# Pacing one queue's gathers and scatters in a fused attention and expert kernel

## The chip, the cores and the metric

The kernel runs on one core of a Trainium2 chip. The metric is the device time of one execution in microseconds (us); lower is better. The engines are named as in the profile: PE (TensorE; PEld is its weight load), DVE (VectorE), ACT (ScalarE), POOL (GpSimd) and SP (SyncE, which here issues most of the transfers).

## The reference

Two blocks run one after the other. The first is attention in which a query sees only the keys of its own cluster. The second sends every token to one of eight experts. Cut to what matters:

```python
# q, k, v: (4, 8, 768, 64); centroids: (8, 16, 64)
q_assign = argmax(normalized(q) @ normalized(centroids).T)   # same for k
mask = q_assign[..., :, None] == k_assign[..., None, :]
scores = where(mask, q @ k.T / sqrt(D), -1e9)
x = softmax(scores) @ v                                # -> (3072, 512)
logits = normalized(x) @ normalized(expert_emb).T / tau  # 8 experts
e = argmax(logits)
gate = softmax(logits)[e]
out = gate * (relu(x @ w1[e]) @ w2[e])                 # w1 512x1024, w2 1024x512
```

## The kernel before, in words

**Attention.** The loop runs over 16 pairs of heads (4 batches b times 4 pairs nb) and, within each, six iterations `it`. An iteration handles two units, each a block of keys against 384 queries of both heads. It makes the scores of the two units ahead (L571, into PSUM tiles `s_ps`), takes their exponentials on ACT (L582, into one of six tiles `prob`), and multiplies the exponentials of its own two units with the values (L593). DVE adds the exponentials up (L612), POOL spreads inverse sums (L664). Finished rows go to a DRAM tensor `x_rows` in transfers that SP issues (L703).

**Early experts.** Tokens of the first batches are known before attention ends. The kernel forms four "early" items E0[0] to E0[3] of 128 tokens each and works them while the last routing is done. A table `early`, keyed by (b, nb, it), says in which iteration a piece of this is recorded. `fetch(E0[0])` gathers the first item with one instruction; for the other three, `early_lot(j, n, behind)` issues the next n of the four gathers of item j. Each gather (L1144, an indirect DMA on POOL) brings 128 pieces of 512 bytes, 64 KB, into an `xin` tile. If `behind` is given, POOL first copies one element of it, so that the gathers are held until that tile has been written. After attention, `hidden(item, (half,))` multiplies with w1 (L1386, tile `h_ps`) and evicts half of `hT` on ACT (L1393); `result` multiplies with w2 (L1426) and ACT scales by the gate into `y` (L1437), which POOL scatters to the output (L1155). `turn_x` transposes a gathered item on DVE (L1262). `fetch_gate` gathers the gates of the early items.

**Routing of the rest.** Beside the early items the last batch is routed: `choose` picks experts, `pb.ranks` (from L873), `pb.dest`, `pb.hot_blocks` and their successors place the tokens. POOL's L1024 is one step of it, read by PE in L1040.

**Later items.** `later` holds sixteen items, numbered 0 to `LAST` = 15: "block" items of 128 tokens and "sized" ones, called wide here, of 160 to 272 tokens of one expert each. The wide item of number i = 12 has six 32-token pieces, that of i = 14 has five; i = 13 and i = 15 are blocks. For a wide item, `sized_hidden` makes eight tiles of hidden features (L1293), evicted by ACT into `hTs` (L1300); `sized_result` makes the output columns (L1331), which DVE transposes into `ys` (L1340) and scales (L1355). `sends` gives the scatters of `ys`, one per piece, 64 KB each (L1155). A list `queue` holds due gathers and scatters of all items. `pump(n, behind)` issues the next n behind a one-element copy on POOL (`pace`, L1683); `share(i, left, behind)` calls it with an n that spreads what is due over the slots that are left.

**The conditional region.** Within block i = 13, between the two halves of its `result`, `overflow` records a branch (L1732) on a value that is loaded on each engine. Its body handles tokens that fit in no item. With these inputs the body is skipped.

**Order.** The order on every engine is the order in which the program records instructions; nothing is reordered by a scheduler. Each engine works its own list in order and waits on semaphores of the others. [...]

Of the kernel before, what the change touches and what calls it, by code (L numbers as in the profile page):

```python
# [9 lines left out]
F32 = mybir.dt.float32  # L10
# [29 lines left out]
def kernel(  # L40
# [12 lines left out]
    nc = tc.nc  # L53
# [4 lines left out]
    F = moe_w1.shape[2]  # L58
    N = B * S
    NJ = S // P  # L60
    NHP = H // 2
# [85 lines left out]
    smp = ctx.enter_context(tc.tile_pool(name="smp", bufs=2))  # L147
# [7 lines left out]
    at = ctx.enter_context(ExitStack())  # L155
# [387 lines left out]
    un = [dict() for _ in units]  # L543
# [597 lines left out]
    mo = {}  # L1141
# [35 lines left out]
    def expert_of(it):  # L1177
        table = {"early": e_early, "sized": e_sized, "block": e_block, "whole": e_block}[it.kind]
        return nc.values_load(
            table[0:1, it.j : it.j + 1], engines=(EngineType.SP,), min_val=0, max_val=E - 1  # L1180
        )

    def weights1(it, parts=1):
        it.e = expert_of(it)
        for i in range(parts):
            load_part(w1s[it.slot], moe_w1, it.e, KD, i, parts)
# [5 lines left out]
    def load_part(w, x, e, chunks, i, parts):  # L1192
        c = slice(chunks // parts * i, chunks // parts * (i + 1))
        nc.sync.dma_start(
            out=w[:, c], in_=x[ds(e, 1)].rearrange("o (c p) f -> p (o c) f", p=P)[:, c]
        )
# [49 lines left out]
    def turn_x(it, evict=None, xT=None):  # L1246
        d = mo[it]
        if it.kind == "sized":
            n = WIDE[it.j]
            d["xT"] = szp.tile([P, KD, SQ * max(WIDE)], F32, tag="xTs", name="xTs")  # L1250
            for u in range(0, n, NQ):
                m = min(NQ, n - u)
                nc.vector.transpose(
                    d["xT"][:, :, SQ * u : SQ * u + SQ * m].rearrange(
                        "p c (w t) -> p w c t", t=SQ
                    ),
                    d["xs"][:, u : u + m].rearrange("p w (c i) -> p w c i", i=SQ),
                )
            return
        d["xT"] = mop.tile([P, DM], F32, tag="xTm", name="xTm") if xT is None else xT  # L1260
        if it.kind == "block" or it in E0[1:]:
            nc.vector.transpose(  # L1262
                d["xT"].rearrange("p (c w t) -> p w c t", c=KD, t=SQ),
                d["xin"].rearrange("p w (c i) -> p w c i", i=SQ),
            )
            return
        bk = psX.tile([P, DM], F32, tag="x_ps", name="x_ps")
        for c in range(KD):
            nc.tensor.transpose(
                bk[:, P * c : P * c + P], d["rows"][:, c].rearrange("p w i -> p (w i)"), ident  # L1270
            )
        evict(d["xT"], bk)
# [86 lines left out]
    def sends(it):  # L1359

        u0, ys = FIRST[it.j], mo.pop(it)["ys"]
        return [
            lambda u=u: scatter(
                out_pieces, flat(spidx)[:, u0 + u : u0 + u + 1], ys[:, u], NQ * N
            )
            for u in range(WIDE[it.j])
        ]

    def flat(t):
        return t.rearrange("p k w -> p (k w)")  # L1370

    def hidden(it, halves=(0, 1)):

        d = mo[it]
        for half in halves:
            if half == 0:
                d["hT"] = (
                    flat(szp.tile([P, KF, max(CAPS)], F32, tag="hTs", name="hTs", bufs=1))[:, 0:F]
                    if it.kind == "whole"
                    else mop.tile([P, F], F32, tag="hT", name="hT")  # L1380
                )
            f0 = 512 * half
            bk = psH.tile([P, 512], F32, tag="h_ps", name="h_ps")
            for m in range(0, 512, P):
                for c in range(KD):
                    nc.tensor.matmul(  # L1386
                        bk[:, m : m + P],
                        lhsT=w1s[it.slot][:, c, f0 + m : f0 + m + P],
                        rhs=d["xT"][:, P * c : P * c + P],
                        start=(c == 0),  # L1390
                        stop=(c == KD - 1),
                    )
            nc.scalar.activation(d["hT"][:, f0 : f0 + 512], bk, ACTF.Relu)  # L1393
# [21 lines left out]
    def result(it, halves=(0, 1)):  # L1415
# [44 lines left out]
        (3, 2, 3): lambda: fetch(E0[0]),  # L1460
        (3, 2, 5): lambda: order_x(E0[0]),
        (3, 3, 1): pa.spread_pieces,
        (3, 3, 2): lambda: early_lot(1, 2),
        (3, 3, 3): lambda: early_lot(1, 1),
        (3, 3, 4): lambda: early_lot(1, 1),
        (3, 3, 5): lambda: early_lot(2, 1),
    }
    early_jobs = {}

    def early_lot(j, n, behind=None):  # L1470

        if j not in early_jobs:
            early_jobs[j] = fetches(E0[j])
        if behind is not None:
            nc.gpsimd.tensor_copy(pace, behind)
        for job in early_jobs[j][0:n]:
            job()
        del early_jobs[j][0:n]
# [9 lines left out]
    E0 = items[0:KA]  # L1488
    later = items[KA:]
# [70 lines left out]
    with tc.manual_schedule(engines=by_hand):  # L1560
        begin()
        for i in range(0, len(units), 2):
            n, it = divmod(i // 2, NJ)
# [18 lines left out]
            b, nb = divmod(n, NHP)  # L1582
# [36 lines left out]
        pace = mop.tile([1, 1], F32, tag="pace", name="pace", bufs=1)  # L1619
# [2 lines left out]
        pb = Places(1, rtb)  # L1622
        gates = gate_pieces(0, B - 1)
        gates[0]()
        early_lot(2, 1)
        logits(0)
        hidden(E0[0], (0,))
        turn_x(E0[1])
# [6 lines left out]
        gates[1]()  # L1635
        gates[2]()
        hidden(E0[0], (1,))
        turn_x(E0[2])
        gates[3]()
        early_lot(3, 2, mo[E0[0]]["hT"][0:1, F - 1 : F])  # L1640
        weights1(E0[2])
        read(0, NJ, P - SQ, P)
        products(1)
        hidden(E0[1], (0,))
        logits(1)
        choose()
        early_lot(3, 2, mo[E0[1]]["hT"][0:1, 511:512])
        hidden(E0[1], (1,))
        weights1(E0[3])
        pb.ranks()  # L1650
        pb.firsts()
# [22 lines left out]
        queue = []  # L1674
# [6 lines left out]
        def pump(n, behind=None):  # L1681
            if n and queue and behind is not None:
                nc.gpsimd.tensor_copy(pace, behind)  # L1683
            queue.sort(key=lambda j: j[0])
            for due, job in queue[0:n]:
                job()
            del queue[0:n]

        def share(i, left, behind=None):

            due = len([j for j in queue if j[0] <= i])
            pump(max(-(-due // left), -(-len(queue) // (left + 3))), behind)
# [59 lines left out]
        LAST = len(later) - 1  # L1752
# [4 lines left out]
        for i, it in enumerate(later):  # L1757
            if i == LAST - 1:
                weights1(later[LAST])
                weights2(later[LAST])  # L1760
            wide = it.kind == "sized"
            if wide:
                order_w2(it)
            if i > 1 and i + 1 < len(later):
                turn_x(later[i + 1])
            made = None
            if i > 0 and later[i - 1].kind == "sized":
                made = mo[later[i - 1]]["ys"][0:1, 0, 0:1]
                queue.extend((min(i + 1, LAST - 2), f) for f in sends(later[i - 1]))
            if 0 < i < LAST - 1 and later[i + 2].kind == "sized":  # L1770
                jobs_of(later[i + 2], i)
            for k in range(i + 2, i + 4):
                if wide and block(k) and later[k] not in mo:
                    jobs_of(later[k], i)
            if wide:
                sized_hidden(it, lambda f, x: share(i, 7 - f // 2, x) if f % 2 else None)
                if i == 1:
                    turn_x(later[2])
                if i + 2 < LAST:
                    weights1(later[i + 2])  # L1780
                    weights2(later[i + 2])
                sized_result(it, lambda g, x: share(i, 3 - g, x) if g < 3 else None)
            elif i < LAST:
                share(i, 3, made)
                hidden(it, (0,))
                share(i, 2, mo[it]["hT"][0:1, 511:512])
                hidden(it, (1,))
                share(i, 1, mo[it]["hT"][0:1, F - 1 : F])
                if i == 0:
                    turn_x(later[1])  # L1790
                    pb.gates(slot_gates)
                if i + 2 < LAST:
                    weights1(later[i + 2])
                result(it, (0,))
                if i == LAST - 2:
                    overflow()
                result(it, (1,))
                if i == 0:
                    jobs_of(later[2], 1)
                    spread_gates()  # L1800
                if i + 2 < LAST:
                    weights2(later[i + 2])
            else:
                pump(len(queue))
                nc.gpsimd.drain()  # L1805
                hidden(it)
                result_last(it)
# [43 lines left out]
```

## Time and profile before

| what | us |
|---|---|
| median of three runs | 698.12 (696.0 to 698.7) |
| the profiled execution, time | 695.11 |
| the profiled execution, span | 693.0 |
| PE busy in the span | 682.6 |
| DVE busy | 382.8 |
| ACT busy | 262.2 |
| POOL busy | 275.6 |

The profile is of one execution. Its page gives busy times, the costliest groups of instructions and the chain that ended last. The trace behind it answers further questions: waits (who waited for whom, in total, how often, longest), timelines (start, duration, engine, line, operation, count, and in brackets the idle time before with what ended it), and stretches of time with the busy time of each engine, the number of its instructions, the clock granted to PE as a share of full speed (1.00 in all stretches but the last), the share of time in which the DMA engines were busy and the rate in GB/s. Line numbers are those of the kernel before. The scatter or gather instruction on POOL is 1.0 us long in the page (56 scatters at 997 ns, 56 gathers at 1013 ns); the copy of one element is 0.18 us. "POOLq" and the like is an engine's sequencer, and "remote" is a wait whose end the trace can't put down to an instruction.

Attention ends at about 325 us of the span, the early items run from there to about 392, and the block with the conditional region is worked from 640 to 660.

### The profile page before, as it was taken

How to read it: one execution, taken by the hardware profiler on the slowest of the kernel's cores; microseconds unless marked ns; L12 is line 12 of the kernel's file. 1: busy time of each engine (PE TensorE's matmuls, PEld its weight loads, DVE VectorE, ACT ScalarE, POOL GpSimd, SP SyncE). 2: the span in 40 equal slices, each digit the busy share in tenths (PEclk: the TensorE clock that was granted, in tenths of full speed). 3: DMA queues.
4: the chain of work that ended last, by engine and by line, in shares of the span. 5: the costliest groups of instructions: out<-in, count | busy, mean ns of one | idle time of the engine just before them, and what ended most of it. 6: DMA issues, size and time to landing. Idle time of an engine off the chain costs nothing. (4 is left out here: it accounts for less than half of the span.)

```text
span 693.0 us, 16339 instructions
## 1 busy us (share of the span) xinstructions
PE 682.6 (99%) x6521; PEld 460.4 (66%) x6521; DVE 382.8 (55%) x673; ACT 262.2 (38%) x444; POOL 275.6 (40%) x505
## 2 busy tenths in 40 slices
PE   8999999999999999999999999999999999999987
PEld 4544444444544444445866678888979797979785
DVE  6898998999899999997674122140301203030310
ACT  6665665576566765574242120101010101111011
POOL 2221222322131222343526343676756465647403
PEclk9999999999999999999999999999999999999999
DMA  9757755776678687689699957457787686878630
GB/s 147 121 82 116 114 100 86 153 141 106 108 131 163 139 147 142 171 209 292 175 311 388 372 189 268 147 175 279 281 282 280 202 301 231 306 249 310 242 133 33
DMA packets 244956, 135.55 MB, mean 196 GB/s; under 512 B 208640, under 2 KB 208642, under 8 KB 244876
## 3 DMA queue, kind: packets, MB, share of 16 engines
q1 hardware_dynamic: 238540, 121.29, 65.0%
q0 software_dynamic: 6160, 13.12, 5.6%
q8 instruction: 53, 0.87, 0.5%
q14 instruction: 27, 0.22, 0.1%
q10 hardware_dynamic: 176, 0.05, 0.0%
HBM read 115.93 MB, written 13.12 MB: 186 GB/s over the span
## 5 line engine op out<-in xcount | busy, mean ns | idle before, releaser
L582 ACT ACTIVATE prob<-s_ps 128x768 f32<-128x768 f32 x192 | 154.0, 814 | 104.7 <-PE s_ps L571 98.6
L571 PE MATMUL s_ps<-qT,kT 64*64 64x384 f32 x1536 | 156.9, 483 | 0.0
L593 PE MATMUL o_ps<-prob,v 64*64 64x385 f32 x1536 | 143.3, 484 | 0.6 <-issue 0.6
L612 DVE TENSOR_TENSOR acc<-acc,prob 128x768 f32<-128x768 f32 x128 | 121.5, 949 | 8.9 <-ACT prob L582 0.5
L593 PEld LDWEIGHTS o_ps<-prob,v 64*64 64x64 f32 x1536 | 58.6, 133 | 66.4 <-issue 58.1
L1340 DVE STREAM_TRANSPOSE ys<-y_ps 128x256 f32<-128x256 f32 (+4 forms) x16 | 6.1, 403 | 154.4 <-PE y_ps L1331 126.6
L1386 PEld LDWEIGHTS h_ps<-xTm,w1s 128*128 128x128 f32 x768 | 87.3, 192 | 2.0 <-issue 1.6
L1386 PE MATMUL h_ps<-xTm,w1s 128*128 128x128 f32 x768 | 88.3, 276 | 0.0
L571 PEld LDWEIGHTS s_ps<-qT,kT 64*64 64x64 f32 x1536 | 55.7, 133 | 35.9 <-issue 31.7
L1426 PE MATMUL y_ps<-w2s,hT 128*128 128x512 f32 x176 | 77.8, 594 | 0.3 <-PEq L1732 0.3
L1293 PE MATMUL h_ps<-xTs,w1s 128*128 128x272 f32 (+7 forms) x384 | 72.9, 346 | 1.8 <-ACT hTs L1300 1.8
L627 POOL COPY behind<-acc 1x1 f32<-1x1 f32 x30 | 6.7, 222 | 168.3 <-DVE acc L612 159.5
L1293 PEld LDWEIGHTS h_ps<-xTs,w1s 128*128 128x128 f32 x384 | 66.7, 190 | 8.6 <-issue 2.9
L1393 ACT ACTIVATE hT<-h_ps 128x512 f32<-128x512 f32 x24 | 14.3, 596 | 147.3 <-PE h_ps L1386 107.8
L1155 POOL DMA_INDIRECT out_dram<-ys,spidx x56 | 55.8, 997 | 33.9 <-issue 19.5
L571 PE MATMUL s_ps<-hot 64*64 64x384 bf16 x768 | 64.6, 325 | 0.1
L1144 POOL DMA_INDIRECT xs<-x_rows,gpidx x56 | 56.8, 1013 | 18.7 <-issue 18.7
L1426 PEld LDWEIGHTS y_ps<-w2s,hT 128*128 128x128 f32 x176 | 32.5, 190 | 37.4 <-issue 36.3
L571 PEld LDWEIGHTS <-hot 64*64 64x64 bf16 x768 | 24.2, 106 | 43.4 <-issue 41.5
L1331 PE MATMUL y_ps<-hTs,w2o 128*128 128x272 f32 (+7 forms) x256 | 48.0, 346 | 0.0
L1331 PE MATMUL misc<-hTs,w2o 128*128 128x272 f32 (+7 forms) x256 | 48.0, 346 | 0.0
L664 POOL COPY inv<-inv 32x12 f32<-32x12 f32 x120 | 31.5, 262 | 36.8 <-DVE inv L661 32.6
(285 smaller groups left out, 740.3 us busy)
## 6 DMA issues: line engine op xcount, KB each, us to landing
w1s<-in_moe_w_dram SPq DMA_DIRECT2D x18, 2048.0 KB
w2s<-in_moe_w_dram SPq DMA_DIRECT2D x18, 2048.0 KB
q<-in_q_dram SPq DMA_DIRECT2D x64, 96.0 KB
k<-in_k_dram SPq DMA_DIRECT2D x64, 96.0 KB
v<-in_v_dram SPq DMA_DIRECT2D x120, 48.0 KB
x_rows<-xb SPq DMA_DIRECT2D x60, 96.0 KB
xr<-x_rows SPq DMA_DIRECT2D x9, 512.0 KB
w1s<-in_moe_w_dram SPq DMA_DIRECT2D x4, 1024.0 KB
```

The lines of the kernel that those rows point to most:

```text
L571: nc.tensor.matmul(s_ps[D * half : D * half + D, h, 0:HS], lhsT=l[rows, half], rhs=r[rows], start=part == (1 if len(parts) < 2 else 0), st ...
L582: nc.scalar.activation(d["prob"][:, :, 0:HS], d["s_ps"][:, :, 0:HS], ACTF.Exp, scale=scale)
L593: nc.tensor.matmul(g["o_ps"][D * h : D * h + D, half, 0:HE], lhsT=ld[n]["v"][keys, j, h], rhs=d["prob"][keys, h, 0:HE], start=(j == 0), st ...
L612: nc.vector.tensor_tensor(g["acc"], g["acc"], d["prob"][:, :, 0:HS], ALU.add)
L664: nc.gpsimd.tensor_copy(inv2[M * to : M * to + M, :, i % 2], inv[M * i : M * i + M])
L1144: nc.gpsimd.indirect_dma_start(out=to, out_offset=None, in_=of, in_offset=bass.IndirectOffsetOnAxis(ap=at, axis=0), bounds_check=n - 1, oo ...
L1155: inst = nc.gpsimd.indirect_dma_start(out=to, out_offset=bass.IndirectOffsetOnAxis(ap=at, axis=0), in_=of, in_offset=None, bounds_check=n - 1,
L1293: nc.tensor.matmul(bk, lhsT=w1s[it.slot][:, c, P * f : P * f + P], rhs=d["xT"][:, c, 0:C], start=(c == 0), stop=(c == KD - 1),)
L1331: nc.tensor.matmul(bks[g][:, 0:C], lhsT=d["w2"][:, f, P * g : P * g + P], rhs=d["hT"][:, f, 0:C], start=(f == 0), stop=(f == KF - 1),)
L1386: nc.tensor.matmul(bk[:, m : m + P], lhsT=w1s[it.slot][:, c, f0 + m : f0 + m + P], rhs=d["xT"][:, P * c : P * c + P], start=(c == 0), stop ...
L1393: nc.scalar.activation(d["hT"][:, f0 : f0 + 512], bk, ACTF.Relu)
L1426: nc.tensor.matmul(bk, lhsT=d["hT"][:, P * c : P * c + P], rhs=w2s[it.slot][:, c], start=(c == 0), stop=(c == KF - 1),)
```

## The change

The change moves gathers and scatters on POOL to other places and puts copies ahead of some of them.

- In the last attention iterations, item 1's four gathers are recorded in iterations 2 to 5, one in each, and each behind a copy that reads the `prob` tile of the first of the iteration's own units. Before, they were recorded as 2, 1 and 1 in iterations 2, 3 and 4, without a copy.
- The first two gathers of item 2 were recorded in iteration 5 and right after attention. All four now go in two pairs, behind the first and the second half of item 0's `hT`.
- Item 3's pairs stood behind item 0's second half and item 1's first half. They now stand behind item 1's first and second half.
- The transpose of item 2 moves behind `choose` on DVE.
- Of the six scatters of the wide item i = 12, two stay in block i = 13, ahead of the region, and four fall due in the wide item i = 14, where `share` spreads them behind its `hTs` tiles. The two later `share` calls of block i = 13 go.
- The copies of `early_lot` write a small tile of a pool that exists in attention, `behind`, and no longer `pace`.

```diff
@@ -1460,11 +1460,13 @@
         (3, 2, 3): lambda: fetch(E0[0]),
         (3, 2, 5): lambda: order_x(E0[0]),
         (3, 3, 1): pa.spread_pieces,
-        (3, 3, 2): lambda: early_lot(1, 2),
-        (3, 3, 3): lambda: early_lot(1, 1),
-        (3, 3, 4): lambda: early_lot(1, 1),
-        (3, 3, 5): lambda: early_lot(2, 1),
+        **{(3, 3, it): lambda it=it: early_lot(1, 1, ahead(3, 3, it)) for it in (2, 3, 4, 5)},
     }
+
+    def ahead(b, nb, it):
+
+        return un[2 * (NJ * (NHP * b + nb) + it)]["prob"][0:1, 0, 0:1]
+
     early_jobs = {}
 
     def early_lot(j, n, behind=None):
@@ -1472,7 +1474,8 @@
         if j not in early_jobs:
             early_jobs[j] = fetches(E0[j])
         if behind is not None:
-            nc.gpsimd.tensor_copy(pace, behind)
+            at = smp.tile([1, 1], F32, tag="behind", name="behind", bufs=1)
+            nc.gpsimd.tensor_copy(at, behind)
         for job in early_jobs[j][0:n]:
             job()
         del early_jobs[j][0:n]
@@ -1622,7 +1625,6 @@
         pb = Places(1, rtb)
         gates = gate_pieces(0, B - 1)
         gates[0]()
-        early_lot(2, 1)
         logits(0)
         hidden(E0[0], (0,))
         turn_x(E0[1])
@@ -1635,17 +1637,18 @@
         gates[1]()
         gates[2]()
         hidden(E0[0], (1,))
-        turn_x(E0[2])
         gates[3]()
-        early_lot(3, 2, mo[E0[0]]["hT"][0:1, F - 1 : F])
+        early_lot(2, 2, mo[E0[0]]["hT"][0:1, F - 1 : F])
         weights1(E0[2])
         read(0, NJ, P - SQ, P)
         products(1)
         hidden(E0[1], (0,))
         logits(1)
         choose()
+        turn_x(E0[2])
         early_lot(3, 2, mo[E0[1]]["hT"][0:1, 511:512])
         hidden(E0[1], (1,))
+        early_lot(3, 2, mo[E0[1]]["hT"][0:1, F - 1 : F])
         weights1(E0[3])
         pb.ranks()
         pb.firsts()
@@ -1766,7 +1769,8 @@
             made = None
             if i > 0 and later[i - 1].kind == "sized":
                 made = mo[later[i - 1]]["ys"][0:1, 0, 0:1]
-                queue.extend((min(i + 1, LAST - 2), f) for f in sends(later[i - 1]))
+                due = LAST - 1 if i == LAST - 2 else min(i + 1, LAST - 2)
+                queue.extend((due, f) for f in sends(later[i - 1]))
             if 0 < i < LAST - 1 and later[i + 2].kind == "sized":
                 jobs_of(later[i + 2], i)
             for k in range(i + 2, i + 4):
@@ -1781,11 +1785,16 @@
                     weights2(later[i + 2])
                 sized_result(it, lambda g, x: share(i, 3 - g, x) if g < 3 else None)
             elif i < LAST:
-                share(i, 3, made)
+                if i == LAST - 2:
+                    pump(2, made)
+                else:
+                    share(i, 3, made)
                 hidden(it, (0,))
-                share(i, 2, mo[it]["hT"][0:1, 511:512])
+                if i < LAST - 2:
+                    share(i, 2, mo[it]["hT"][0:1, 511:512])
                 hidden(it, (1,))
-                share(i, 1, mo[it]["hT"][0:1, F - 1 : F])
+                if i < LAST - 2:
+                    share(i, 1, mo[it]["hT"][0:1, F - 1 : F])
                 if i == 0:
                     turn_x(later[1])
                     pb.gates(slot_gates)
```

## The prediction

> **What bounds the kernel now.** I read the page's engine totals first, then TensorE's own list of waits, then the timelines of the two places that the change touches.
>
> ```profile
> PE 682.6 (99%) x6521; PEld 460.4 (66%) x6521; DVE 382.8 (55%) x673; ACT 262.2 (38%) x444; POOL 275.6 (40%) x505
> ```
>
> TensorE (PE) is busy for 682.6 of 693.0 us. POOL issues every gather and scatter and is 40% busy. So an edit to POOL's order can only pay where PE stands still or runs below its own rate. Both touched places have such a spot. The first is the end of attention; PE's waits between 280 and 420 us are two:
>
> ```profile
> PE x_ps L1269 <- ACT prob L582: 0.9, 1, 0.9
> PE o_ps L593 <- issue: 0.6, 1, 0.6
> ```
>
> The timelines there, POOL, PE and ACT in turn:
>
> ```profile
> 316.59 1.00 POOL L1144 DMA_INDIRECT xin<-x_rows,early_i  x1 [0.30 <-issue]
> 317.89 1.00 POOL L1144 DMA_INDIRECT xin<-x_rows,early_i  x1 [0.30 <-issue]
> 319.19 1.00 POOL L1144 DMA_INDIRECT xin<-x_rows,early_i  x1 [0.30 <-issue]
> ```
> ```profile
> 317.08 1.52 PE L571 MATMUL s_ps<-qT,kT 64*64 64x384 f32 x8
> 318.10 2.31 PE L593 MATMUL o_ps<-prob,v 64*64 64x385 f32 x13
> 320.98 0.87 PE L593 MATMUL o_ps<-prob,v 64*64 64x385 f32 x3 [0.57 <-issue]
> 322.71 0.63 PE L1269 MATMUL x_ps<-ident,rows 128*128 128x128 f32 x4 [0.86 <-ACT prob L582]
> ```
> ```profile
> 321.06 1.51 ACT L582 ACTIVATE prob<-s_ps 128x768 f32<-128x768 f32 x2 [3.77 <-remote]
> ```
>
> The eight score matmuls take 1.52 us here and 0.81 or 0.82 us in every group before; the sixteen L593 matmuls take 3.75 us (318.10 to 321.85) instead of 1.46; the exponential at 321.06 starts 3.77 us after ACT fell idle, though its scores were done by 317.1. From 317.08 to the next group, at 324.72, is 7.64 us. At the pitch of the neighbours (0.65 + 1.30 + 0.56 + 1.45) it is 3.96. PE lost **3.7 us**, most of it counted as busy. POOL issues six gathers without a break just then (312.32 to 320.19), and the transfers are dense. Density alone doesn't do it, as two stretches of 4 us show (PE's matmuls are the first number in brackets; DMA share and GB/s are last):
>
> ```profile
> 304.00:308.00 4.00, 4.00 (x64) 2.02 (x60) 3.59 (x8) 2.38 (x5) 1.89 (x5) 1.00 1.03 381
> ...
> 316.00:320.00 4.00, 4.00 (x39) 1.66 (x37) 1.46 (x2) 1.29 (x3) 3.09 (x4) 1.00 1.04 374
> ```
>
> 64 matmuls against 39, at equal transfer. The gathers are what differs most visibly; the trace does not prove them the cause.
>
> The second place is the conditional region, L1732. POOL, ACT and PE:
>
> ```profile
> 650.49 0.98 POOL L1155 DMA_INDIRECT out_dram<-ys,spidx  x1 [0.57 <-issue]
> 651.77 0.97 POOL L1155 DMA_INDIRECT out_dram<-ys,spidx  x1 [0.30 <-DVE xTm L1262]
> 660.64 0.98 POOL L1155 DMA_INDIRECT out_dram<-y,sidx  x1 [7.90 <-ACT hTs L1300]
> ```
> ```profile
> 659.68 0.69 ACT L1437 ACTIVATE y<-y_ps,slot_gates 128x512 f32<-128x512 f32 x1 [10.07 <-DMA xin<-x_rows,gpidx]
> ```
> ```profile
> 654.33 3.42 PE L1293 MATMUL h_ps<-xTs,w1s 128*128 128x160 f32 x24
> 657.59 1.25 PE L1293 MATMUL x_ps<-xTs,w1s 128*128 128x160 f32 x8
> 660.61 3.53 PE L1293 MATMUL h_ps<-xTs,w1s 128*128 128x160 f32 x24 [1.77 <-ACT hTs L1300]
> ```
>
> and what POOL did in its 7.9 us, from the view of line L1732:
>
> ```profile
> L1732 POOLq EVENT_SEMAPHORE  x5: 17/42/43, 651.9 to 658.0; - x5
> ...
> L1732 POOLq INC_SWDGE_SEM  x1: 1390/1390/1390, 658.1 to 658.1; - x1
> ```
>
> The program, read from its instructions: on the path that skips the region, POOL waits until all it has sent has landed, then raises the semaphores as the skipped body would have (1.39 us, to 659.46). ACT's y waits for those semaphores and starts at 659.68. The label "xin" on its wait is an inference of the view; POOL's semaphore step is what ended just before. With y stuck, the four hTs tiles behind it on ACT stay in PSUM, and PE waits **1.77 us**.
>
> [...] the scatter at 651.77 lasts 0.97 us, and POOL is held until 658.0. [...] The trace shows up to 6.2 (651.77 to 658.0) beside weight loads, and I use 6.2. [...]
>
> **The change, part by part.** The sums are against the profiled execution: 695.11 us, 693.0 of it span. The median of the three runs, 698.12, is 3.0 above it; I carry the difference over.
>
> *Scatters.* Of six scatters of the last-but-one wide item, those at 643.36 and 644.70 stay ahead of the region; four go, with four copies of 0.18 us, behind hTs tiles 1, 3, 5, 7 of the item after it. POOL loses two pace copies ahead of the region and gains four behind it. The second scatter lands by 644.70 + 6.2 = 650.9, POOL's step ends at 652.3. ACT's y needs its matmuls, done at 650.82 + 3.67 = 654.49. So POOL is 2.2 us early, y starts at about 654.5 and hTs at 655.2, and PE's wait goes: **-1.8 us**. From there PE runs unbroken to 688, so the end moves with it. What is late next is the scores' own pace, no wait. The four scatters cost POOL 4 x (0.18 + 0.5 gap + 1.0) = 6.7 us between about 656 and 665, where it idles until 675.4. Their 262 KB are 0.7 us of DMA at the 389 GB/s of this stretch. The last weights, issued at 654.52, are needed at 679 and the DMA share is 0.06 from 670 to 680, so ten us cover this. Cost 0; without that cover, 0.7. The output buffer of the wide item behind the region is not the one that the four scatters read, so its transposes don't wait for them.
>
> *Gathers in attention.* Six in a row become four, each behind a copy that reads the score tile of its turn. POOL is inside L664 until 312.05, so the first three still go at about 312.8, 314.5 and 316.1 (0.18 copy, 0.5 gap, 1.0 each). The fourth waits for the exponential at 321.06 (or 317.9, if that is no longer held). The other two leave the stretch. I take half of the 3.7 us: **-1.8 us**, bounds -3.7 (the burst is all of it) and 0 (weights and row stores are). A loss is bounded by the cover: the gather lands at worst at 322.6 + 1.0 + 5 = 328.6; the transpose that reads it, now at 327.17, has 2.37 us of idle behind it on DVE, to 330.20. One new wait: the exponential that rewrites the first tile waits for POOL's read, done by 312.6 against 317.1. Cost 0.
>
> *Gathers of items 2 and 3.* Item 2's four go at the two existing turns, 330.77 and 336.43. Item 3's move one turn later, and its last pair goes behind the second hT half of item 1, at 342.7. That pair now issues at 343.9 and 345.2, so the four gate gathers behind it on POOL start at 346.5 instead of 343.51. ACT's y of item 0 waits for the first: 343.51 to 350.26 is 6.75 us, so 353.3. Its scatter then starts at 354.2 and POOL's L1024 at 355.5, ending 357.1. PE reads that at 359.54 (L1040): 2.4 us cover. Cost 0; each us beyond is one us.
>
> *Moved transpose.* On DVE item 2's transpose (0.71) moves behind ten small operations, to just before L873. DVE idles 4.42 us there; gathers issued by 338.8 must land by 341.5 for it. The pair issued then before had the same time. Gates come 0.2 to 0.4 us earlier. Taken as 0. SP's and PE's orders are the same in both programs. POOL gains seven copies, 1.3 us, in idle time.
>
> Sum: -1.8 - 1.8 = -3.6. Profiled 691.5; median **694.5**.
>
> **The rivals.** About 0.5%, 3.5 us, is what a measurement of this kernel can tell from no change.
> 1. *Both places pay*, with about half or more of the 3.7: 692.6 to 694.6, centre 694.5. For it: equal transfer, different matmul rate. Against: three gathers still come close together. 0.46.
> 2. *Only the region pays*; attention's end is held by the weight loads and row stores that the change leaves: 698.1 - 1.8 = 696.3, with a little from attention 695. For it: ACT was already 1.37 us late at 315.87, with two gathers issued. 0.36.
> 3. *Nothing moves*: y at 654.5 is held by another of its semaphores, or PE waits a little later: 698. Against: y starts 0.2 us after POOL's step. 0.06.
> 4. *Slower*: the delayed gate gathers reach PE. The place is L1040 at 359.54, through ACT's y and POOL's L1024. It starts to cost from a gate landing of 6.75 + 2.4 = 9.2 us. To end 3.5 us slower, with the region's gain alone, PE must stand 5.3 us, a landing of 14.5: 701.6. For it: rows are being read back there, and the 6.75 is long. Against: that reading thins out at 350. 0.12.
>
> **How the numbers follow.** Faster 0.46, same 0.36 + 0.06, slower 0.12. The forecast is rival 1's, 694.5; its own range is 692 to 695. Low end: 692.6, less 1.1 for the spread of the runs (696.0 to 698.7). High end: 698.1 for rival 3, plus 0.9. That leaves out rival 4 and some of each tail.
>
> **What would show it.** Right: no wait of PE on L1300's tiles near 659 and ACT's y at about 652 to 655; more than 39 matmuls in the 4 us from 316, and ACT's wait ahead of the last exponentials under 2 us; L1040 without a wait. Wrong: the 3.7 us at the same place with four gathers (rival 2); y still after POOL's step (3); a new PE wait between 355 and 365 (4).

## The result, and the profile after

| | median, us | runs |
|---|---|---|
| before | 698.49 | 6, 696.0 to 699.3 |
| after | 690.33 | 6, 690.0 to 692.3 |

The ratio is 0.9891, with a 95% interval of 0.9873 to 0.9910: 8.2 us faster. The forecast was 694.5, and its range ended at 691.5. The profiled execution of the changed kernel took 690.58 us with a span of 688.4; that of the kernel before took 695.11 with 693.0. So 4.6 us of the 8.2 can be looked for in the two traces. Most of the rest, 3.4 us, is that the median of the kernel before lies that far above its profiled execution. Later runs on five chips show what the number depends on: the changed kernel takes about 690 us on the two where it ran, the kernel before 695.2 to 695.8 on three and 690 on the other two.

The engine totals on the page of the changed kernel:

```profile
PE 681.5 (99%) x6521; PEld 459.7 (67%) x6521; DVE 384.0 (56%) x673; ACT 262.7 (38%) x444; POOL 277.4 (40%) x512
```

In TensorE's list of waits both waits near the end of attention and the wait on `hTs` (1.77 us before) are gone; the largest one left is 1.1 us at the start of the program.

**End of attention.** The timelines of POOL, PE and ACT of the changed kernel:

```profile
312.87 1.03 POOL L1144 DMA_INDIRECT xin<-x_rows,early_i  x1 [0.15 <-POOL behind L1478]
314.74 1.17 POOL L1144 DMA_INDIRECT xin<-x_rows,early_i  x1 [0.15 <-issue]
316.95 1.02 POOL L1144 DMA_INDIRECT xin<-x_rows,early_i  x1 [0.16 <-issue]
319.32 1.02 POOL L1144 DMA_INDIRECT xin<-x_rows,early_i  x1 [0.54 <-issue]
```
```profile
317.52 0.81 PE L571 MATMUL s_ps<-qT,kT 64*64 64x384 f32 x8
318.17 1.46 PE L593 MATMUL o_ps<-prob,v 64*64 64x385 f32 x16
319.56 0.66 PE L1269 MATMUL x_ps<-ident,rows 128*128 128x128 f32 x4
320.14 1.52 PE L593 MATMUL o_ps<-prob,v 64*64 64x385 f32 x16
321.60 0.62 PE L722 MATMUL misc<-xT,embT 128*32 128x96 f32 x20
```
```profile
317.65 1.57 ACT L582 ACTIVATE prob<-s_ps 128x768 f32<-128x768 f32 x2 [1.27 <-POOL behind L1478]
```

The eight score matmuls take 0.81 us and the sixteen L593 matmuls 1.46, as everywhere else. From the last score group to L722 it is 321.60 - 317.52 = 4.08 us; before it was 324.72 - 317.08 = 7.64. **3.56 us are gained here.** I call this the stretch below. ACT's wait fell from 3.77 to 1.27 us. The copy named as its releaser ended at 316.8, the scores that ACT takes only at 317.5, so it is the scores that it waits for. Of the four copies on POOL only the last waited for its tile (0.62 us); the second and the third lasted 0.67 and 0.87 us instead of 0.18. That is how the gathers came to start 1.9 to 2.4 us apart, where before it was 1.3 to 1.6. The window beside the one of before that the prediction shows (PE's matmuls in the first bracket, DMA share and GB/s last):

```profile
316.00:320.00 4.00, 4.00 (x48) 1.71 (x44) 3.96 (x4) 2.56 (x6) 2.67 (x4) 1.00 1.05 379
```

PE has 48 matmuls in it instead of 39, and DVE works 3.96 of 4 us instead of 1.46, at much the same 379 GB/s (374 before).

**The region.** POOL, ACT and PE, and POOL's semaphore step on the skipped path (L1732 before, now L1735):

```profile
640.85 1.03 POOL L1155 DMA_INDIRECT out_dram<-ys,spidx  x1 [0.16 <-issue]
642.18 1.00 POOL L1155 DMA_INDIRECT out_dram<-ys,spidx  x1 [0.30 <-issue]
```
```profile
652.09 0.69 ACT L1437 ACTIVATE y<-y_ps,slot_gates 128x512 f32<-128x512 f32 x1 [6.86 <-PE y_ps L1426]
```
```profile
651.84 3.42 PE L1293 MATMUL h_ps<-xTs,w1s 128*128 128x160 f32 x24
655.10 1.25 PE L1293 MATMUL x_ps<-xTs,w1s 128*128 128x160 f32 x8
656.18 3.42 PE L1293 MATMUL h_ps<-xTs,w1s 128*128 128x160 f32 x24
```
```profile
L1735 POOLq INC_SWDGE_SEM  x1: 1310/1310/1310, 644.5 to 644.5; - x1
```

POOL raises the semaphores from 644.5 to 645.8 and y now waits for nothing but its own matmuls. As the prediction reads the program, POOL's step starts when all that it has sent has landed; by that reading the second scatter (642.18) took at most 2.3 us. PE's three groups follow each other without a gap: **1.77 us gained**. The two places make 5.3 us; about 0.7 us is given back in small pieces elsewhere, 0.4 of it ahead of the stretch, where the two programs are the same.

### The profile page after: what moved, and what is told of

It is laid out like the page before. It is cut to its first block, busy times and chain, and to the rows that moved or that the text cites. A ratio compares the mean times of both kernels' runs of the same rounds, so it can differ in the third digit from the quotient of the medians.

```text
span 688.4 us, 16351 instructions
## 1 busy us (share of the span) xinstructions
PE 681.5 (99%) x6521; PEld 459.7 (67%) x6521; DVE 384.0 (56%) x673; ACT 262.7 (38%) x444; POOL 277.4 (40%) x512
## 5 line engine op out<-in xcount | busy, mean ns | idle before, releaser
L593 PE MATMUL o_ps<-prob,v 64*64 64x385 f32 x1536 | 141.5, 484 | 0.0
L593 PEld LDWEIGHTS o_ps<-prob,v 64*64 64x64 f32 x1536 | 58.0, 133 | 65.2 <-issue 57.1
```

What stands on the lines that cost most here:

```text
L593: nc.tensor.matmul(g["o_ps"][D * h : D * h + D, half, 0:HE], lhsT=ld[n]["v"][keys, j, h], rhs=d["prob"][keys, h, 0:HE], start=(j == 0), st ...
```

## The experiments

The runs were made on five chips, named P to T here (the letters A to D in the expectations are theories). The kernel before took 695.2 us on P, 695.8 on Q, 695.6 on R, 690.0 on S and 690.4 on T. The chip of the pair above is not on record. Each chip was used once, P to T in this order, so a difference between chips can't be told from one between times.

### Which part pays (chip P)

**Scatters alone.** The kernel before with the two edits of the scatters:

```diff
-                queue.extend((min(i + 1, LAST - 2), f) for f in sends(later[i - 1]))
+                due = LAST - 1 if i == LAST - 2 else min(i + 1, LAST - 2)
+                queue.extend((due, f) for f in sends(later[i - 1]))
...
-                share(i, 3, made)
+                if i == LAST - 2:
+                    pump(2, made)
+                else:
+                    share(i, 3, made)
...
```

> Only the move of the four scatters behind the region, the rest as before. Theory A (the end of attention pays most of the 8.2 us: 3.6 shown by the two profiles, and more in the ordinary runs of before, which are 3.4 us above its profiled run): this run gains 1.8 us against before, ratio 0.997 to 0.998. Theory B (the part that the two profiles don't show lies in the region, where the landing of scatters varies from run to run): this run gains 4 to 6 us, ratio 0.991 to 0.994. Both: no wait of PE on ACT at L1293 in its profile.

693.45 us against 695.24, ratio 0.9978 (0.9969 to 0.9986): 1.8 us, as theory A had it. PE's wait in the region is gone, the stretch lasts 7.56 us (317.61 to 325.17).

**Early gathers alone.** The changed kernel with the scatters as before (the first diff the other way round).

> Only the edits of the early items, the scatters as before. Theory A: a gain of about 6.4 us, ratio near 0.991, and the runs lie closer together than those of before. Theory B: a gain of about 3.6 us, ratio near 0.995, with the scatter of before's runs kept. Both: the 1.8 us wait of PE at L1293 stays.

690.66 us, ratio 0.9938 (0.9925 to 0.9951): 4.6 us, where theory A had 6.4 and theory B 3.6. In its trace the stretch is 4.08 us, and PE's wait in the region is kept at 1.61:

```profile
657.16 3.53 PE L1293 MATMUL h_ps<-xTs,w1s 128*128 128x160 f32 x24 [1.61 <-ACT hTs L1300]
```

With the run before, theory A holds in that the end of attention pays most. Its 6.4 counted on a kernel before of 698.5 us; on this chip it takes 695.2. The 4.6 are 1.0 more than the 3.56 of the stretch. The traced run took 691.67 us, itself 1.0 above the median of its six and 3.4 below the traced run of before in the first pair, about what the stretch gives. Four of the six took 690.4 to 690.8 and have no trace, so where the last 1.0 us comes from stays open.

**Four gathers, not held.** The changed kernel with its gathers in the same iterations, but without the copies:

```diff
-        **{(3, 3, it): lambda it=it: early_lot(1, 1, ahead(3, 3, it)) for it in (2, 3, 4, 5)},
+        **{(3, 3, it): lambda it=it: early_lot(1, 1) for it in (2, 3, 4, 5)},
```

> The changed kernel without the four copies in attention: item 1's four gathers are recorded in the same iterations, but nothing holds them, so they go in a row from 312.5. Theory C (what slows PE is gathers issued without a pause): the loss comes back for the most part, 2 to 3 us slower than the changed kernel in the profile (span 690.5 to 691.5), PE's matmuls at the end of attention thin out again. Theory D (what matters is the number of gathers in the stretch, four and not six): as the changed kernel within 0.5 us, ratio 0.989.

690.53 us, ratio 0.9934 (0.9920 to 0.9948). The four gathers go in a row at 312.80, 314.14, 315.77 and 317.07, and the stretch is 4.85 us: 0.8 of the 3.6 is back, less than theory C had and more than theory D. The changed kernel was not run on this chip, so this rests on the trace.

**Six gathers, held.** The kernel before with the copies put on its own lots:

```diff
-        (3, 3, 2): lambda: early_lot(1, 2),
+        (3, 3, 2): lambda: early_lot(1, 2, ahead(3, 3, 2)),
...
-        (3, 3, 5): lambda: early_lot(2, 1),
+        (3, 3, 5): lambda: early_lot(2, 1, ahead(3, 3, 5)),
```

> Before, with copies alone: the lots of before (2, 1, 1 for item 1 and 1 for item 2 in attention, one right after) each behind a copy of the turn's score tile; scatters and the rest as before. Theory C (pauses): most of the early gain comes with these copies, about 4 to 6 us against before, ratio 0.991 to 0.995. Theory D (number): five gathers in attention still, so little gain, ratio 0.997 to 1.0.

691.93 us, ratio 0.9958 (0.9943 to 0.9972): 3.3 us, again between C and D. Four gathers go at 312.5 to 317.8, then POOL waits 1.54 us for a score tile and the last two go from 320.1. The stretch is 4.89 us. Six gathers with one pause cost as little as four in a row. So neither the number alone nor the pause alone decides: a row of six without a pause costs 3.6 us, and either a shorter row or a pause takes most of that away.

### The row or the dense transfers (chip Q)

**The change again**, beside the kernel before:

> The changed kernel as it is, beside the four runs of its parts. If the two parts simply add (scatters alone 1.8 us, early gathers alone 4.6 us), it stands 6.0 to 6.6 us below the kernel before, near 689 us on a chip where the kernel before takes 695.2. If they hide one another or part of it is lost again (the end of the kernel takes over), it stands at 4.3 to 5.2 us below, level with the early gathers alone. If the first comparison's 8.2 us belongs to the change and not to that pair of runs, it is 8 us again.

690.05 us against 695.77, ratio 0.9916 (0.9899 to 0.9932): 5.7 us, between the two sums that were expected. The 8.2 us of the first pair don't come back, and it is the kernel before that differs.

**Fewer weights beside the row.** Scatters alone, with the two w2 loads of the second early item moved out of the stretch:

```diff
-            (15, 1): (w2s, 1, 0),
-            (15, 2): (w2s, 1, 1),
...
+        weights2(E0[1])
         weights1(E0[2])
```

> The kernel before with the scatter edits, its six gathers in an unbroken row kept at the end of attention, but the two 1 MB loads of the second early item's w2 leave that stretch: they go as one load ahead of the third item's w1, where DMA is less dense. C (a row of gathers slows PE only beside dense transfers): the 24 matmuls of the last groups take 0.81 and 1.46 us again instead of 1.08 and 2.34, ACT's wait ahead of the last exponentials falls from 3.7 us to under 2, the loss falls under 1 us, and the time falls by 3 us or more against scatters alone unless a matmul then waits for w2. D (the row of gathers alone does it): the loss stays at 3 to 3.7 us, ACT's wait over 3 us, and the time is that of scatters alone or worse.

699.76 us, ratio 1.0065: slower, because PE now waits 4.0 us for the third item's w1 behind the moved load. The mean granted clock of its four runs is 0.994 to 0.996; in the eighteen of the kernel before on this chip it is 0.998 to 1.000, but for two at 0.995. The reading is in the stretch. Its windows (matmuls first, DMA share and GB/s last):

```profile
316.00:318.00 2.00, 2.00 (x24) 0.95 (x23) 0.45 (x1) 0.77 (x3) 1.42 (x2) 1.00 0.58 109
318.00:320.00 2.00, 1.77 (x13) 0.54 (x9) 0.18 (x1) 0.00 (x0) 1.67 (x2) 1.00 1.10 174
320.00:322.00 2.00, 1.77 (x13) 0.25 (x8) 2.00 (x1) 0.69 (x1) 0.33 (x1) 1.00 0.21 55
```

The rate fell from 375 GB/s to 109, 174 and 55, and PE is as slow as before; the stretch lasts 7.76 us (317.22 to 324.98), ACT waits 4.54. While the loss lasts, dense transfers are not needed. For the four us ahead of it, where the first gathers go, this is not shown; the next run has 162 and 220 GB/s around its first gathers.

**A second row elsewhere.** The changed kernel with six more gathers in the middle of attention, their result unused:

`spare_row(n)` issues n gathers into two spare input tiles.

```diff
+        (2, 2, 3): lambda: spare_row(6),
...
+            for w in range(n // 2):
+                gather(to[:, w], x_pieces[0 : NQ * P], io_i[:, 8 * w + lot : 8 * w + lot + 1], NQ * P)
```

> The changed kernel with six more gathers in an unbroken row in the middle of attention, near 219 us, where POOL is idle for 9 us: 128 pieces of 512 bytes each as in the row at the end of attention, into two spare input tiles, read from the first rows of x_rows by a constant index (every partition the same piece), their result unused. No weights are being loaded there (150 to 220 GB/s against 380). C (a row hurts only beside dense transfers): PE keeps 60 to 64 matmuls in each 4 us from 216 to 232, ACT has no wait over 2 us that it does not have in the changed kernel, and the time is within 0.5 us of it. D (the row alone hurts): some 3 us are lost at that place, PE's groups of 0.81 and 1.46 us grow to over 1.0 and over 2.3, and the time is 3 us longer.

695.07 us, where the changed kernel takes 690.05 on this chip: **5.0 us lost**. The traced run is one of the longest of the fifteen, 697.66 us. Windows, and ACT's timeline:

```profile
220.00:224.00 4.00, 4.00 (x60) 1.80 (x50) 3.69 (x11) 2.17 (x4) 3.08 (x4) 1.00 1.24 220
224.00:228.00 4.00, 2.60 (x21) 0.91 (x19) 3.86 (x7) 0.95 (x2) 2.38 (x4) 1.00 1.12 147
228.00:232.00 4.00, 4.00 (x30) 1.65 (x27) 1.45 (x4) 3.48 (x6) 0.94 (x1) 0.57 0.97 145
```
```profile
225.62 0.81 ACT L582 ACTIVATE prob<-s_ps 128x768 f32<-128x768 f32 x1 [3.45 <-PE o_ps L593]
```

The row goes out from 218.64 to 226.8. Until 223 all is well; then an exponential starts at 225.62 that starts at 222.87 without the row, and PE falls from 60 matmuls to 21 and 30. From 228 to 232 the granted clock is 0.57. That is one more loss, and it follows the first.

**The kernel before once more.**

> The kernel before once more, for a second profile. Its runs lie between 693.7 and 699.3 us where the changed kernel's lie within 2.3 us. If the loss at the end of attention is what varies from run to run, a profile with another time than 695.1 us shows another loss there (7.64 us from 317 to the next group in the first), by as much as the time differs; if the variation is elsewhere, this stretch is the same 7.6 us and the time differs.

697.11 us, span 695.0: 2.0 above the first profile. PE's timeline and three windows (the granted clock is the third number from the end):

```profile
323.12 0.94 PE L1269 MATMUL x_ps<-ident,rows 128*128 128x128 f32 x4 [0.86 <-ACT prob L582]
323.98 2.85 PE L593 MATMUL o_ps<-prob,v 64*64 64x385 f32 x16
326.76 0.87 PE L722 MATMUL misc<-xT,embT 128*32 128x96 f32 x32
```
```profile
322.00:324.00 2.00, 1.14 (x8) 0.58 (x7) 1.90 (x3) 1.58 (x4) 0.00 (x0) 0.82 1.03 210
324.00:326.00 2.00, 2.00 (x17) 0.78 (x16) 1.79 (x3) 0.59 (x1) 0.00 (x0) 0.50 0.47 88
326.00:328.00 2.00, 2.00 (x44) 1.10 (x37) 0.80 (x2) 1.09 (x2) 0.00 (x0) 0.83 1.07 276
```

Up to 323.12 the stretch is as in the first profile (5.71 us from the last score group, against 5.63). From there to L722 it takes 3.64 us instead of 2.01, and from 324 to 326 the granted clock is 0.50. Over the three windows the granted clock falls short by 0.18, 0.50 and 0.17 of 2 us each: 1.7 of the 2.0 us is the clock after the stall. So the loss at the end of attention is the same, and what varies is behind it. PE's waits in the stretch are 0.55 and 0.86 us, and the rest counts as busy, with few matmuls (8 in each of the windows from 320 to 322 and from 322 to 324). What lowers the clock behind this stall, and not behind the same one in the first profile, is not shown. Scatters alone, which keep the stall, took 693.1 to 693.7 us in 16 runs and 695.0 to 695.2 in 5, 1.7 apart, and the mean granted clock of those five is 0.997 or 0.998, mostly below that of the others (0.998 to 1.000).

### What makes a row costly (chip R)

All four add gathers or copies to the changed kernel, with `spare_row(n, behind)`, which can now copy one element of `behind` first; their result is unused. The changed kernel itself was not run on this chip. It took 690.05 us on Q and 690.33 in the first pair. Nor was the row of six near 219 us run here: that it would cost something on R too is taken from Q, and from the kernel before, which takes 695.6 on R.

**Three gathers near 219 us.**

```diff
+        (2, 2, 3): lambda: spare_row(3),
```

> The changed kernel with three more gathers in a row near 219 us, where six cost about 5 us; their result is unused. If a row costs in proportion to its gathers, this one costs half: 2.3 to 2.5 us. If the engines only fall behind after the third gather has been sent (in the row of six the exponentials were late from the fourth gather on), three cost under 0.7 us.

690.77 us. PE keeps 60 to 64 matmuls in each 4 us; one exponential starts 0.8 us late (223.64) and nobody waits for it. Against 690.05 to 690.33, three in a row cost 0.4 to 0.7 us, and 0.9 against the shortest of the four runs here.

**Six gathers, one a turn, each behind a copy.**

```diff
+        **{(2, 2, it): lambda it=it: spare_row(1, ahead(2, 2, it)) for it in (3, 5)},
...
+        **{(2, 3, it): lambda it=it: spare_row(1, ahead(2, 3, it)) for it in (1, 2, 3)},
```

> The changed kernel with the same six gathers from 219 us on, but one a turn, each behind a copy that reads the score tile of its turn, as the change does at the end of attention; their result is unused. If what costs is the unbroken row, this costs under 0.7 us, PE keeps 60 to 64 matmuls in each 4 us and ACT is on time. If what costs is the number of gathers, wherever they are, it costs the same 3.8 to 5 us, spread out.

690.33 us: nothing that can be told from none. The gathers start at 219.36, 221.55 and 223.60, and the other three at 233.34, 235.38 and 239.45. So six gathers as such don't cost; the row without a pause does. Whether two us between gathers are enough, or the break of ten us is needed, this does not tell.

**Six plain copies in a row.**

```diff
+            nc.gpsimd.dma_start(out=to, in_=x_pieces[P * k : P * k + P])
```

> The changed kernel with six plain copies (no index list) of 128 x 128 float32 from x_rows in a row on POOL's queue near 219 us, in the place and with the bytes of the six gathers; their result is unused. If what costs is any row of transfers that POOL describes, PE loses 3.8 us or more here too. If it is what an index list needs, or if plain copies take POOL less time, it costs under 0.7 us.

689.84 us: nothing. On POOL the six are short:

```profile
217.88 3.49 POOL L1483 DMA_DIRECT2D spare<-x_rows  x6
```

They take 3.49 us together, and the same 393 KB on the same queue (192 packets on q0 in this run and in that with six gathers) don't disturb PE, which keeps 60 to 67 matmuls in each 4 us. Whether the index lists matter, or the 1.3 us from one gather to the next, this does not tell.

**Six gathers near 86 us, reading `moe_w1`.**

```diff
+        (0, 3, 4): lambda: spare_row(6, ahead(0, 3, 4)),
```

> The changed kernel with six more gathers in a row near 86 us, held by one copy until the score tile of that turn, in a stretch where the 16 DMA engines are 0.15 busy from 88 to 92 us and 0.73 from 92 to 96; they read pieces of 512 bytes of moe_w1, the same one for every partition, and their result is unused. D (the row alone does it): 3.5 us or more are lost within 12 us of the first gather. C, in the form that DMA engines must be busy, if not with many bytes: under 1.5 us, as the six gathers near 219 us fell beside row stores that kept them 0.98 to 1.24 busy.

690.53 us, and no loss in the trace: PE keeps 60 to 64 matmuls in each 4 us from 80 to 104. But these gathers went 1.3 to 2.1 us apart (POOL took 1.4 to 1.8 us for three of them), so the run has both an idler place and a slower row. It does not decide for theory C.

### Length and place (chip S)

> The changed kernel with four more gathers in a row near 219 us (three cost under 1 us there, six about 5), their result unused. If the loss begins with the fourth gather and grows with each, this costs 1 to 2.5 us, as four in a row at the end of attention cost 1 us in the profile. If it takes a longer row, it costs under 0.7 us, as three did.

> The changed kernel with five more gathers in a row near 219 us, their result unused. Growing with each gather from the fourth on: 2.5 to 4 us. A step at one length: either as six (4 to 5 us) or as three (under 0.7 us).

> The changed kernel with six more gathers in a row near 140 us, reading x_rows as the six near 219 us did, their result unused. The 16 DMA engines are 1.03 busy there from 140 to 144 us and 0.87 from 144 to 148, with 230 and 136 GB/s. If a row of six beside other transfers is what costs: 3.5 us or more within 12 us of its first gather. If the place near 219 us is special, or if the gathers come out further apart than 1.3 us again: under 1 us.

> The changed kernel with six more gathers in a row near 219 us, as in the run that cost 5 us, but reading moe_w1, as the six near 86 us did that cost nothing; their result is unused. If the place decides, this costs 4 to 5 us. If the tensor that is read decides, under 1 us.

```diff
+        (2, 2, 3): lambda: spare_row(4),
```

This is the first; five, six at (1, 2, 3), and six that read `moe_w1` are added in the same way. They took 689.80, 689.99, 690.26 and 689.98 us. The kernel before, beside them: 689.98 us in 39 runs. The last run has its six gathers 1.3 us apart near 219 us, as in the run that lost 5.0 us on chip Q, and PE's groups after them are 0.81 and 1.46 us. So these runs tell nothing of length and place: on this chip no row costs anything.

### Before and after where before takes 690 us (chip T)

The two kernels unedited.

> The kernel before, for a third profile. Where it takes about 690 us, the stretch from 317 us to the next group should take about 4 us instead of 7.64, with ACT's wait under 2 us, although the same six gathers go out in a row; PE's wait behind the conditional region (1.6 to 1.8 us) should still be there. Where it takes 695 or more, the stretch shows 3.6 us of loss or more again, and the level of 690 was that one chip's.

> The changed kernel beside it on the same chip. Where the kernel before takes about 690 us: only the region's term is left, 1.5 to 1.8 us faster. Where it takes 695 or more: 5 to 6 us faster, as on the earlier chips.

Before 690.38 us (23 runs, and 690.11 in 12 more), after 689.88: ratio 0.9993 (0.9984 to 1.0002). **Here the change is worth nothing that can be measured.** The 1.5 to 1.8 us that were expected of the region do not show either. The trace of the kernel before on this chip, POOL, PE and ACT at the end of attention, and the window:

```profile
315.61 1.00 POOL L1144 DMA_INDIRECT xin<-x_rows,early_i  x1 [0.30 <-issue]
316.91 0.99 POOL L1144 DMA_INDIRECT xin<-x_rows,early_i  x1 [0.31 <-issue]
318.21 1.00 POOL L1144 DMA_INDIRECT xin<-x_rows,early_i  x1 [0.30 <-issue]
```
```profile
317.40 0.81 PE L571 MATMUL s_ps<-qT,kT 64*64 64x384 f32 x8
318.04 1.46 PE L593 MATMUL o_ps<-prob,v 64*64 64x385 f32 x16
```
```profile
317.48 1.62 ACT L582 ACTIVATE prob<-s_ps 128x768 f32<-128x768 f32 x2 [1.60 <-PE s_ps L571]
```
```profile
316.00:320.00 4.00, 4.00 (x48) 1.71 (x44) 3.96 (x4) 2.23 (x4) 3.08 (x4) 1.00 1.05 391
```

The same six gathers go out 1.3 us apart, the transfers are as dense (391 GB/s), and the stretch is 4.08 us. The region, on ACT, POOL and POOL's sequencer:

```profile
643.89 0.60 ACT L1393 ACTIVATE hT<-h_ps 128x512 f32<-128x512 f32 x1 [2.98 <-PE h_ps L1386]
652.34 0.69 ACT L1437 ACTIVATE y<-y_ps,slot_gates 128x512 f32<-128x512 f32 x1 [7.85 <-DMA xin<-x_rows,gpidx]
```
```profile
646.80 0.97 POOL L1155 DMA_INDIRECT out_dram<-ys,spidx  x1 [0.30 <-POOLq L1732]
```
```profile
L1732 POOLq INC_SWDGE_SEM  x1: 1390/1390/1390, 650.7 to 650.7; - x1
```

y still waits for POOL's step (652.1), but that comes earlier, for two reasons. ACT writes the second half of `hT` 7.3 us after PE began on the tile (636.55); in the first profile it was 9.2 us (639.77 to 649.01), and the last two scatters are held until that tile. And, by the same reading of the program, the last scatter has landed at most 3.9 us after its start (646.80 to 650.7), not 6.3 (651.77 to 658.1). Both together let PE through without a wait.

In the first profile the late tile stood behind a row of four gathers and four scatters, from 637.25 on, in which no copy had to wait. In the changed kernel two scatters are left in that row, and PE begins on the tile at 637.29. The first profile has:

```profile
649.01 0.60 ACT L1393 ACTIVATE hT<-h_ps 128x512 f32<-128x512 f32 x1 [4.87 <-remote]
```

In the changed kernel the same write starts at 644.63, 7.3 us after PE began, and the wait before it is 2.98 us, for PE. From its end to y ACT is idle for 6.86 us there, and just as long in the run with the scatters alone moved. So I read the region's 1.77 us as a loss of the same kind as that in attention: ACT late behind a row of indirect transfers on POOL. It is not shown: the one edit shortens the row and also leaves POOL's step less to wait for.

## Why the prediction was wrong

The forecast of 694.5 lies 4.2 us above the measured 690.33. Of these, 0.9 lie in the profiled execution (691.5 forecast, 690.58 measured) and 3.3 in the step from there to the median.

**The step to the median: this step failed, and it is most of the miss.** I carried over the 3.0 us by which the median of before lay above its profiled run, as if they belonged to both kernels. In the first pair they are 3.4, and after lies 0.25 below its own profiled run: nothing carries over. What those 3.4 us were stays open. The profiled run of before has a granted clock of 1.00 until PE's last work; the second profile, on chip Q, has 1.7 us of clock loss behind the stall, and two runs of before on Q at 698.2 and 698.4 us have a mean granted clock of 0.995 where the others have 0.998 to 1.000. By my estimate, twice the 1.7 us would make up the 3.4 us of the first pair, but no trace of such a run was taken.

**The end of attention, -1.8 us: this step failed, by its size.** I halved a loss of 3.7 us because three gathers still go close together and because weights and row stores stay. The profile gained 3.56, nearly all of it. The first ground fell because the gathers started 1.9 to 2.2 us apart: the copies took up to 0.87 us, where I had counted 0.18. The second fell in the changed kernel, where weights and row stores go on at 379 GB/s and nothing is lost. Nor are the weights needed for the loss: it is the same in the run with the weights moved away, at less than half of the rate, and the row near 219 us cost 5.0 without them. Row stores stood beside both of these rows, so whether they are needed stays open. Timed by itself, that part measured 4.6 us; the 1.0 beyond the stretch is open. The 5 us that I gave a gather for landing, in the bound of a loss, were an estimate; the last of the four starts at 319.32, and the transpose that reads it at 325.01, without a wait.

**The scatters, -1.8 us: right** on the chips with the loss. Alone they measured 1.8, y starts with its own matmuls, PE's wait is gone, and the four scatters behind the region (655.40 to 661.91) delay nobody. What stood behind the number was not seen: I took the landing of 6.2 us as the scatters' own. By the reading of the program, the second of the two that are left took at most 2.3 us (642.18 to 644.5), and on chip T the last of six took at most 3.9. The two places make 5.3 us together, while the profiled executions differ by 4.5; the 0.8 us given back elsewhere is why the profiled forecast is off by 0.9 only, though the halved term was short by 1.8.

**The zeros: right.** The first gate gather starts at 343.15 and y follows at 348.17, 5.0 us later where I had taken 6.75; PE's L1040 starts without a wait at 356.44. The moved transpose of item 2 now waits 2.98 us for its gathers, and DVE is idle 0.93 us after it, so no work moved.

**The rivals.** Rival 1 was the case, beyond its lower end: 5.3 us in its two places are 692.8 from the median of three, inside its 692.6 to 694.6, and the 3.0 us that don't carry over made the rest. Rival 2's ground, ACT 1.37 us late at 315.87 with two gathers issued, speaks for the row too: beside the same weight loads that exponential is on time in the changed kernel (two in a row from 314.12), and so it is with the same gathers on chip T. Rival 4 did not come near. No rival had the chip in it: on T nothing moves, as in rival 3, but because the kernel before loses nothing there.

## What to carry to other kernels

On some of the chips here, a row of indirect gathers without a pause held up PE, ACT and DVE for 3.6 to 5.0 us, most of it counted as busy on PE; look for groups of matmuls that last longer than their twins (1.52 us against 0.81 for the last scores). Break such rows with a small copy behind a tile of the neighbouring work: that cost nothing measurable here, and the changed kernel took 690 us in all three comparisons, beside a kernel before of 698.5, 695.8 and 690.4. When a profiled run and the median differ by more than the runs of a quieter version do, look at the granted clock behind the longest stall (0.50 from 324 to 326 in the second profile of before) before carrying the difference over.

## What the runs showed of the hardware

- The loss depends on the chip, or on something else that changed between the runs on R and those on S. Before took 695 to 698 us in the first pair and on P, Q and R, and 690 on S and T; six gathers in a row cost about 3.6 us or more in the first pair and on P and Q, and nothing on S and T. After took 690.3, 690.05 and 689.9 in the three comparisons.
- In the first pair and on Q and R the views of transfers give no times of landing; on S and T they do. The w1 loads in the page of before, in the first profile and on chip T:

```profile
w1s<-in_moe_w_dram SPq DMA_DIRECT2D x18, 2048.0 KB
```
```profile
w1s<-in_moe_w_dram SPq DMA_DIRECT2D x18, 2048.0 KB, 11.3
```

  So the traces that give these times are those of the two chips without the loss. Whether the one has to do with the other was not tried. What makes a row costly stays open.
- With the loss, a row of six costs 3.6 us (the stretch) to 5.0 us (near 219 us), and PE's loss begins 4 to 5 us after the first gather; three in a row, six with pauses and six plain copies cost 0.9 us or less on chip R, whose kernel before had the loss.
- Two traces have a lower granted clock in the midst of PE's work, over 4 to 6 us: behind the stall in the second profile of before (0.82, 0.50 and 0.83 in windows of 2 us), and behind the row near 219 us (0.60 and 0.55). Each time the shortfall sums to 1.7 us. The first profile of before, with the same stall, has none of it.
